# Hash attention and a squared-ReLU feed-forward: both feed-forward products by halves with seven products

## The chip, the cores and the metric

The kernel runs on one core of a Trainium2 chip. The metric is the device time of one execution in microseconds (us), and lower is better. A core has five engines that run side by side and wait for each other by semaphores: TensorE (PE in the profile, and PEld for its weight loads), VectorE (DVE), ScalarE (ACT), GpSimd (POOL) and SyncE (SP), whose queue issues nearly all transfers here. Products land in PSUM, which TensorE writes and VectorE and ScalarE read; all else lies in SBUF or in DRAM.

## The reference

```python
mask   = q_bucket[:, :, :, None] == k_bucket[:, :, None, :]   # 6 sign bits of q @ proj, k @ proj
scores = scale * q @ k.T;  scores = where(mask, scores, -1e9) - max
attn   = exp(scores) / (sum + 1e-9)
x      = (attn @ v).transpose(0, 2, 1, 3).reshape(3072, 512)   # 4 x 8 heads, 768 x 64
h      = x @ w_in          # 512 x 2048
g      = maximum(h, 0) ** 2
out    = g @ w_out         # 2048 x 512
```

Inputs and the result are float32, the two weights float64.

## The kernel before, in words

**First part, attention.** The 32 heads are worked on as 16 pairs, each pair on 128 partitions (64 a head), and each pair in six steps of 128 keys: 96 steps. A step has on TensorE the scores (`score`, L306: a bf16 product of sign bits that lifts the keys of the same bucket, then the float32 product of features, for queries 0 to 383 and then 384 to 767), one item that prepares the next pair (`features`, `hash_bits`), and the product with the values of the step before last (`attend`, L338). ScalarE takes the exponential (L313) into a ring of eight tiles. VectorE adds them up over the keys (`add_up`, L327, one step later). At the end of a pair `sum_up` (L355, tile `tot`) sums these totals over partitions on TensorE, VectorE makes reciprocals, `spread` (L378) hands them round, and `normalize` (L392) writes the pair's part of x into `x_t`, which holds all of x in SBUF (48 KB a partition), features on partitions.

Beside that the float64 weights come in 32 pieces of 128 x 512, one every three steps: SP loads a piece (`load_weight`), three steps later VectorE, GpSimd and ScalarE take it apart (`part_weight`), and a step after that it is rounded to float32 (`round_weight`; the last operation is a product on GpSimd, L159). `w_in` lies as four blocks of 128 rows, `w_out` as sixteen.

**Second part, feed-forward.** x is taken in six chunks of 512 tokens. The hidden stage of a chunk makes 16 tiles of 128 hidden units x 512 tokens, each from four products (L500), then ScalarE's ReLU out of PSUM (L506) and VectorE's square (L508). The output stage makes four tiles of 128 tokens x 512 features, each from 16 products (L517), copied out by ScalarE (L522) and written by SP. In chunks 1 and 2 VectorE also takes maxima of q and k (`peak`, L468), and in chunk 3 `guard` turns them into a flag (L483): were it set, a general path (`general`) would do all again. It isn't set here.

**What sets the order.** Each engine has a queue and works strictly in the order in which the program was written; the pools of tiles add the waits: a new tile waits until what lay in its memory before has been read.

Of the kernel before, what the change touches and what calls it, by code (L numbers as in the profile page):

```python
# [8 lines left out]
FP32 = mybir.dt.float32  # L9
# [5 lines left out]
ALU = mybir.AluOpType  # L15
# [18 lines left out]
def kernel(  # L34
# [24 lines left out]
    PIECE = 512  # L59
    assert (S, D, DM) == (768, 64, 512) and 3 * NBITS <= D  # L60
# [14 lines left out]
    fast = ExitStack()  # L75


    x_t = fast.enter_context(tc.tile_pool(name="x_all", bufs=1)).tile([P, NFT, B * S], FP32, name="x_t")

    first = ExitStack()  # L80
    p_qk = first.enter_context(tc.tile_pool(name="p_qk", bufs=2))
    p_f = first.enter_context(tc.tile_pool(name="p_f", bufs=2))
    p_w = first.enter_context(tc.tile_pool(name="p_w", bufs=2))
    p_v = first.enter_context(tc.tile_pool(name="p_v", bufs=3))
# [137 lines left out]
    def load_pair(pr, k_queue):  # L222
        b, j = divmod(pr, PB)
        tiles = []
        for src, pool, name in ((q, p_qk, "q_nat"), (k, p_qk, "k_nat"), (v, p_v, "v_nat")):
            pair = src[b, 2 * j:2 * j + 2]
            if src is v:
                t = pool.tile([P, 2, SB * D], FP32, name=name)
                nc.sync.dma_start(out=t, in_=pair.rearrange("h (p t) d -> p h (t d)", t=SB))
            else:  # L230
                t = pool.tile([P, SB, 2, D], FP32, name=name)
                for h in range(2):
                    (k_queue if src is k else nc.sync).dma_start(
                        out=t[:, :, h], in_=pair[h].rearrange("(p t) d -> p t d", t=SB)
                    )
            tiles.append(t)
        nat[pr] = tiles

    def features(pr, w, r):
# [4 lines left out]
        for i in range(SB // 2):  # L244
# [3 lines left out]
                in_=nat[pr][w][:, t].rearrange("p h d -> p (h d)"),  # L248
# [48 lines left out]
    def score(pr, kt):  # L297

        st = [ps_s.tile([P, 2, 512], FP32, name="st") for _ in range(2)]
        key = slice(kt * P, (kt + 1) * P)  # L300
        for c in range(2):
            cut = slice(c * HS, (c + 1) * HS)
            for src, first in ((bits, True), (feat, False)):
                for h in range(2):
                    rows = slice(h * D, (h + 1) * D)
                    nc.tensor.matmul(  # L306
                        out=st[h][:, c, 0:HS], lhsT=src[pr, 1][rows, key],
                        rhs=src[pr, 0][rows, cut], start=first, stop=not first,
                    )
        for h in range(2):  # L310
# [3 lines left out]
                out=e[:, 0:S].rearrange("p (c f) -> p c f", c=2), in_=st[h][:, :, 0:HS],  # L314
                func=ACTF.Exp, scale=scale,
# [15 lines left out]
    def attend(pr, kt):  # L331
        if kt == 0:
            outs[pr] = ps_o.tile([P, 2, 512], FP32, name="xo")
# [383 lines left out]
```

## Time and profile before

| | |
|---|---|
| median of three runs | 1065.76 us (1065.65 to 1066.94) |
| the profiled execution | 1067.2 us |
| its span, first to last instruction | 1065.4 us |
| mean granted clock of TensorE | 0.999 |
| busy: PE, DVE, ACT, POOL | 1046.3, 426.7, 285.0, 116.2 us |
| attention, weights beside it | 0 to 398.8 us |
| feed-forward, twelve stages | 398.9 to 1060.3 us |

A row of a group has the line, engine, operation, the tiles written and read, their shape and the count; behind the first bar the busy time in us and the mean of one in ns, behind the second the idle time of that engine just before and what ended it. A row of the timeline has start and length in us, engine, line, tiles, shape and count, and in brackets the wait. A float32 product is recorded as two passes, so counts of these are twice those in the code.

### The profile page before, as it was taken

Reading aid. Unit: us, or ns where it says so; the run is one execution under the profiler, and the core shown is the slowest. Engines: PE = TensorE matmul, PEld = TensorE weight load, DVE = VectorE, ACT = ScalarE, POOL = GpSimd, SP = SyncE. Lnnn points to the kernel's source line nnn. Section 1 sums busy time; section 2 is a strip of 40 time slices with the busy share of each in tenths; the row PEclk is TensorE's granted clock in tenths of the full one; section 3 lists DMA queues with packets and bytes.
Section 4 is the critical chain, followed back from the end, with each engine's and each line's share of the span. In section 5 each row is a group of like instructions: output and inputs, shape, how many; then the busy total and the mean of one; then the engine's idle time right before and its main releaser. Section 6 shows DMA issues by size and latency. Waiting matters only on the chain.

```text
span 1065.4 us, 10162 instructions
## 1 busy us (share of the span) xinstructions
PE 1046.3 (98%) x4066; PEld 456.0 (43%) x4066; DVE 426.7 (40%) x593; ACT 285.0 (27%) x457; POOL 116.2 (11%) x115
## 2 busy tenths in 40 slices
PE   6999999999999999999999999999999999999998
PEld 3444444444444434444444444444444444444443
DVE  2888888888888882200341034101210011001100
ACT  4555555555555541100110011001100111001100
POOL 1232322333232330000000000000000000000000
PEclk9999999999999999999999999999999999999999
DMA  8233333334421100000420033000000000000000
GB/s 198 81 93 85 85 86 84 85 114 119 104 85 55 61 20 0 1 10 20 157 89 10 20 128 119 10 20 10 1 0 20 20 1 0 20 20 1 0 20 22
DMA packets 65012, 55.24 MB, mean 52 GB/s; under 512 B 51648, under 2 KB 55744, under 8 KB 64960
## 3 DMA queue, kind: packets, MB, share of 16 engines
q1 hardware_dynamic: 63328, 54.14, 17.2%
q8 instruction: 34, 0.56, 0.2%
q10 hardware_dynamic: 1568, 0.39, 0.2%
q14 instruction: 18, 0.15, 0.0%
q0 software_dynamic: 64, 0.00, 0.0%
HBM read 48.24 MB, written 6.29 MB: 51 GB/s over the span
## 4 chain that ended last, share of the span: by engine, by line
PE 93%; DVE 3%; ACT 3%; issue 1%; DMA 1%; SPq 0%; ACTq 0%
PE hid L500 31%; PE y L517 31%; PE st L306 13%; PE xo L338 11%; ACT e L313 2%; PE tp L246 2%; PE near L263 2%; PE tot L355 1%; DVE flip L360 1%; DMA q_nat<-in_q_dram 1%; DVE one L131 0%; DVE power L127 0%; DVE once L366 0%; PE st L263 0%; DVE once L362 0%
## 5 line engine op out<-in xcount | busy, mean ns | idle before, releaser
L500 PE MATMUL hid<-x_t,w_in 128*128 128x512 f32 x768 | 330.8, 592 | 0.0
L517 PE MATMUL y<-w_out,gate 128*128 128x512 f32 x768 | 330.6, 592 | 0.0
L508 DVE TENSOR_TENSOR gate<-r 128x512 f32<-128x512 f32 x96 | 66.5, 692 | 508.9 <-ACT r L506 506.8
L517 PEld LDWEIGHTS y<-w_out,gate 128*128 128x128 f32 x768 | 145.9, 190 | 183.7 <-issue 183.4
L500 PEld LDWEIGHTS hid<-x_t,w_in 128*128 128x128 f32 x768 | 145.8, 190 | 183.3 <-issue 183.3
L313 ACT ACTIVATE e<-st 128x768 f32<-128x768 f32 x192 | 144.6, 805 | 89.3 <-PE st L306 89.3
L306 PE MATMUL st<-feat,feat 64*128 64x384 f32 x768 | 158.7, 485 | 0.0
L327 DVE TENSOR_TENSOR total<-total,e 128x768 f32<-128x768 f32 x128 | 145.6, 1186 | 1.5 <-ACT e L313 1.5
L338 PE MATMUL xo<-e,v_nat 128*64 128x384 f32 (+1 forms) x768 | 145.0, 499 | 0.0
L506 ACT ACTIVATE r<-hid 128x512 f32<-128x512 f32 x96 | 57.3, 597 | 275.4 <-PE hid L500 275.4
L522 ACT COPY o<-y 128x512 f32<-128x512 f32 x24 | 14.1, 586 | 315.7 <-PE y L517 315.7
L306 PEld LDWEIGHTS st<-feat,feat 64*128 64x128 f32 x768 | 69.4, 188 | 27.7 <-issue 27.2
L306 PE MATMUL st<-bits,bits 64*128 64x384 bf16 x384 | 71.7, 326 | 3.8 <-ACT e L313 1.9
L338 PEld LDWEIGHTS xo<-e,v_nat 128*64 128x64 f32 x768 | 46.6, 136 | 65.6 <-issue 65.5
L306 PEld LDWEIGHTS <-bits 64*128 64x128 bf16 x384 | 20.2, 93 | 69.3 <-issue 56.6
L327 DVE TENSOR_TENSOR total<-e,e 128x768 f32<-128x768 f32 x32 | 45.3, 1459 | 7.0 <-ACT e L313 7.0
L136 POOL TENSOR_SCALAR power<-power 128x512 uint32<-128x512 uint32 x32 | 22.9, 716 | 199.6 <-DVE power L127 199.6
L142 ACT ACTIVATE one<-one 128x512 f32<-128x512 uint32 x32 | 20.2, 630 | 84.9 <-DVE one L131 84.9
L159 POOL TENSOR_TENSOR w_in<-one,power 128x512 f32<-128x512 f32 x16 | 30.7, 1919 | 42.1 <-DVE one L156 42.1
L159 POOL TENSOR_TENSOR w_out<-one,power 128x512 f32<-128x512 f32 x16 | 30.0, 1878 | 41.2 <-DVE one L156 41.2
L251 ACT COPY feat<-tp 128x384 f32<-128x384 f32 x64 | 31.0, 484 | 5.4 <-PE tp L246 5.4
L139 POOL TENSOR_SCALAR power<-power 128x512 uint32<-128x512 uint32 x32 | 29.1, 910 | 2.6
(69 smaller groups left out, 373.0 us busy)
## 6 DMA issues: line engine op xcount, KB each, us to landing
raw<-in_moe_w_in_dram SPq DMA_DIRECT2D x16, 512.0 KB, 4.3
raw<-in_moe_w_out_dram SPq DMA_DIRECT2D x16, 512.0 KB, 3.8
q_nat<-in_q_dram SPq DMA_DIRECT2D x32, 192.0 KB, 5.1
v_nat<-in_v_dram SPq DMA_DIRECT2D x16, 384.0 KB, 3.2
out_dram<-o SPq DMA_DIRECT2D x24, 256.0 KB, 2.0
raw_qk<-in_q_dram SPq DMA_DIRECT2D x8, 768.0 KB, 4.2
raw_qk<-in_k_dram SPq DMA_DIRECT2D x8, 768.0 KB, 4.1
k_nat<-in_k_dram SPq DMA_DIRECT2D x30, 192.0 KB, 5.1
```

The costliest lines, as they stand in the source:

```text
L136: nc.gpsimd.tensor_scalar(out=power, in0=power, scalar1=1151.0, scalar2=896.0, op0=ALU.min, op1=ALU.max,)
L139: nc.gpsimd.tensor_scalar(out=power, in0=power, scalar1=-896.0, scalar2=2.0**23, op0=ALU.add, op1=ALU.mult,)
L159: nc.gpsimd.tensor_tensor(out=pieces[i][3], in0=one, in1=power.bitcast(FP32), op=ALU.mult)
L251: nc.scalar.copy(out=feat[pr, w][:, r * HS:(r + 1) * HS], in_=tp[:, 0:HS])
L306: nc.tensor.matmul(out=st[h][:, c, 0:HS], lhsT=src[pr, 1][rows, key], rhs=src[pr, 0][rows, cut], start=first, stop=not first,)
L313: nc.scalar.activation(out=e[:, 0:S].rearrange("p (c f) -> p c f", c=2), in_=st[h][:, :, 0:HS], func=ACTF.Exp, scale=scale,)
L327: nc.vector.tensor_tensor(out=totals[pr, h], in0=in0, in1=weights[pr, kt, h][:, 0:S], op=ALU.add)
L338: nc.tensor.matmul(out=xo[h * D:(h + 1) * D, c, 0:n], lhsT=nat[pr][2][:, h, kt * D:(kt + 1) * D], rhs=weights[pr, kt, h][:, c * HS:c * HS ...
L500: nc.tensor.matmul(out=hp, lhsT=w_in[:, ft, ff * P:(ff + 1) * P], rhs=x_t[:, ft, i * NCH:(i + 1) * NCH], start=(ft == 0), stop=(ft == NFT ...
L506: nc.scalar.activation(out=r, in_=hp, func=ACTF.Relu)
L508: nc.vector.tensor_tensor(out=g, in0=r, in1=r, op=ALU.mult)
L517: nc.tensor.matmul(out=y, lhsT=gates[ff][:, n * P:(n + 1) * P], rhs=w_out[:, ff], start=(ff == 0), stop=(ff == NFF - 1),)
```

## The change

**Second part.** Every operand is cut into halves both ways, and a product of two such operands is made from seven products of quarter blocks instead of eight, with sums of blocks ahead and sums of products behind. For the left operand these sums are S1 = A21 + A22, S2 = S1 − A11, S3 = A11 − A21, S4 = A12 − S2 (written over A21); for the right one T1 = B12 − B11, T2 = B22 − T1, T3 = B22 − B12, T4 = B21 − T2 (over B12). The seven products go into three accumulators of 256 columns, two of each kind: accumulator 0 takes A11·B11, S2·T2, S3·T3 and A22·T4 one after another, and ScalarE copies it out after each of the first three (`one`, `two`, `three`) before the next is added; accumulator 2 takes S1·T1, is copied (`five`), and then S4·B22; accumulator 1 holds A12·B21. VectorE adds the copies to make the four result blocks.

For x and w_in this gives four gate tiles of 128 x 256 per row of blocks (eight rows a chunk), and VectorE then makes the sums of the gates for the output product. GpSimd makes the sums of the weights: for `w_in` two rows of blocks near the end of attention (`sums_in`) and the other six in the first chunk, for `w_out` (`sums_out`) all eight in the first chunk. VectorE makes those of x (`load_x`). Since S4 and T4 are written over quarters of the weights, these quarters are first copied to DRAM (`kept_in`, `kept_out`) for the general path. The maxima of q and k come in sixteen pieces each of 768 columns over chunks 1 to 4, `guard` after the hidden stage of the last chunk.

**x through DRAM.** Each pair's x is normalized by one operation into a small tile and written to `x_all` in DRAM; a chunk of 512 tokens is read back by one transfer of 1 MB, the first while attention still runs, each other at the end of the hidden stage before.

**Attention.** Passes of 512 and 256 columns in place of two of 384 (scores) and 512 and 257 in place of 384 and 385 (output); the values are loaded one pair ahead into two buffers instead of three; weight pieces come every 2.7 steps instead of 3.

```diff
+    x_all = p_d.tile([P, NFT, B * S], FP32, name="x_all")
+    kept_in = p_d.tile([P, NFT // 2, DFF // 2], FP32, name="kept_in")
+    kept_out = p_d.tile([P, NFF // 2, DM // 2], FP32, name="kept_out")
...
-        for c in range(2):
-            cut = slice(c * HS, (c + 1) * HS)
+        for lo, hi in CUTS:
             for src, first in ((bits, True), (feat, False)):
...
-        for c in range(2):
-            cut = slice(c * HS, (c + 1) * HS)
-            nc.vector.scalar_tensor_tensor(
-                out=x_t[:, j, b * S + c * HS:b * S + (c + 1) * HS],
-                in0=xo[:, c, 0:HS], scalar=xo[:, 1, HS:HS + 1],
-                in1=recs[pr][:, cut], op0=ALU.add, op1=ALU.mult,
-            )
+        nc.vector.scalar_tensor_tensor(
+            out=x_t, in0=xo[:, 0:S], scalar=xo[:, S:S + 1],
+            in1=recs[pr], op0=ALU.add, op1=ALU.mult,
+        )
+        nc.sync.dma_start(out=x_all[:, j, b * S:(b + 1) * S], in_=x_t)
+
+    def sums_a(e, a11, a12, a21, a22, s1, s2, s3):
+        e.tensor_tensor(out=s1, in0=a21, in1=a22, op=ALU.add)
+        e.tensor_tensor(out=s3, in0=a11, in1=a21, op=ALU.subtract)
+        e.tensor_tensor(out=s2, in0=s1, in1=a11, op=ALU.subtract)
+        e.tensor_tensor(out=a21, in0=a12, in1=s2, op=ALU.subtract)
...
-    EVERY = 3
+    when = [27 * i // 10 for i in range(len(pieces))]
+    ROUNDED = when[-1] + 5
...
+            if u == ROUNDED:
+                early.close()
+                nc.sync.dma_start(out=kept_in, in_=w_in[:, 0:2, HF:DFF])
+                nc.sync.dma_start(out=kept_out, in_=w_out[:, 0:NR, HD:DM])
...
+                def load_x(i):
+                    x = p_c.tile([P, NFT, NCH], FP32, name="x")
+                    nc.sync.dma_start(out=x, in_=x_all[:, :, i * NCH:(i + 1) * NCH])
...
+                    sums_b(
+                        nc.vector, x[:, 0:2, lo], x[:, 0:2, hi], x[:, 2:4, lo], x[:, 2:4, hi], *t_x
+                    )
+                load_x(0)
+            if ROUNDED < u <= ROUNDED + 2:
+                sums_in(u - ROUNDED - 1)
...
+        def product(n, at, bt, c11, c12, c21, c22):
+            acc = [ps_m.tile([P, 512], FP32, name=f"acc{i}")[:, 0:HN] for i in range(3)]
...
+            add(0, at["11"], bt["11"], True, False)
+            one = keep(0, "one")
+            add(1, at["12"], bt["21"], True, True)
+            c11(acc[1], one)
+            add(0, at["s2"], bt["t2"], False, False)
+            two = keep(0, "two")
+            add(2, at["s1"], bt["t1"], True, False)
+            five = keep(2, "five")
+            add(0, at["s3"], bt["t3"], False, False)
+            three = keep(0, "three")
+            add(2, at["s4"], bt["22"], False, True)
+            c12(acc[2], two)
+            c22(three, five)
+            add(0, at["22"], bt["t4"], False, True)
+            c21(acc[0])
...
+            def gate(out):
+                def put(one, two=None):
+                    h = p_r.tile([P, HN], FP32, name="h", bufs=4)
+                    if two is None:
+                        nc.scalar.copy(out=h, in_=one)
+                    else:
+                        nc.vector.tensor_tensor(out=h, in0=one, in1=two, op=ALU.add)
+                    nc.vector.scalar_tensor_tensor(
+                        out=out, in0=h, scalar=0.0, in1=h, op0=ALU.max, op1=ALU.mult
+                    )
+                return put
+            product(2, at, bt, gate(g["11"]), gate(g["21"]), gate(g["12"]), gate(g["22"]))
+            sums_a(
+                nc.vector, g["11"], g["12"], g["21"], g["22"], g["s1"], g["s2"], g["s3"]
+            )
...
         for i in range(NCHUNK):
+            for r in range(NR):
+                if i == 0 and r + 2 < NR:
+                    sums_in(r + 2)
+                if i == 0:
+                    sums_out(r)
+                hidden(i, r)
+                if i > 0 and i < 5:
+                    peak(i % 2, (i - 1) // 2 * NR + r)
+            if i == NCHUNK - 1:
+                guard()
+            if i + 1 < NCHUNK:
+                load_x(i + 1)
+            for m in range(2):
+                project(i, m)
```

`keep` is a ScalarE copy out of an accumulator, `add` the products of one of the seven (two for a hidden block, eight for an output block), `project` the output product with `product(NR, ...)`.

Three places show how the instructions move. On TensorE, at the border of the two parts: before, the last `attend` of the last pair and then whole stages.

```order
L378 MATMUL tot<-both,picks 128x24
L338 MATMUL xo<-e_108,v_nat 64x384
L338 MATMUL xo<-e_109,v_nat 64x384
L338 MATMUL xo<-e_108,v_nat 64x385
L338 MATMUL xo<-e_109,v_nat 64x385
L500 MATMUL hid<-x_t,w_in 128x512 x64
L517 MATMUL y<-w_out,gate 128x512 x64
```

Now, at the same place, the first hidden row of blocks (`acc_3454`, `acc_3455` and `acc_3456` are its accumulators 0, 1 and 2; `t_x` and `s_in` are sums of x and of w_in):

```order
L344 MATMUL xo<-e_115,v_nat 64x257
L344 MATMUL xo<-e_116,v_nat 64x257
L534 MATMUL acc_3454<-x,w_in 128x256 x2
L534 MATMUL acc_3455<-x,w_in 128x256 x2
L534 MATMUL acc_3454<-t_x_3218,s_in_118 128x256 x2
L534 MATMUL acc_3456<-t_x_3217,s_in_117 128x256 x2
L534 MATMUL acc_3454<-t_x_3219,s_in_119 128x256 x2
L534 MATMUL acc_3456<-x,w_in 128x256 x2
L534 MATMUL acc_3454<-x,w_in 128x256 x2
L534 MATMUL acc_3510<-x,w_in 128x256 x2
```

Four products of 512 columns per hidden tile have become fourteen of 256 per row of blocks, which answers to two tiles; the first of them has a wait for the last normalization, since its accumulator lies where the attention output lay.

On VectorE, in pair 14 (steps 3 to 5): before, between the hash bits of pair 15 and the end of the pair.

```order
L270 TENSOR_SCALAR bits_2905<-far,bars,gains 64x384 x2
L127 TENSOR_SCALAR power<-raw 128x512
L131 TENSOR_SCALAR one<-raw 128x512
L327 TENSOR_TENSOR total_2835<-total_2835,e_104 128x768
L327 TENSOR_TENSOR total_2836<-total_2836,e_105 128x768
L152 SCALAR_TENSOR_TENSOR power<-raw,power 128x512
L156 SCALAR_TENSOR_TENSOR one<-raw,one 128x512
L327 TENSOR_TENSOR total_2835<-total_2835,e_106 128x768
```

Now:

```order
L279 TENSOR_SCALAR bits_3164<-far,bars,gains 64x384 x2
L160 SCALAR_TENSOR_TENSOR power<-raw,power 128x512
L164 SCALAR_TENSOR_TENSOR one<-raw,one 128x512
L334 TENSOR_TENSOR total_3084<-total_3084,e_115 128x768
L334 TENSOR_TENSOR total_3085<-total_3085,e_116 128x768
L417 TENSOR_TENSOR t_x_3217<-x 128x512
L418 TENSOR_TENSOR t_x_3219<-x 128x512
L419 TENSOR_TENSOR t_x_3218<-x,t_x_3217 128x512
L420 TENSOR_TENSOR x<-x,t_x_3218 128x2x256
L334 TENSOR_TENSOR total_3084<-total_3084,e_109 128x768
L334 TENSOR_TENSOR total_3085<-total_3085,e_110 128x768
```

The last rounding of a weight (L160, L164) has moved up to here, and the four sums of the first x chunk stand between the totals; the first of them waits for that chunk's transfer.

On GpSimd, at the end of the weights: before, the product of the last piece was the end of its work. Now that product is followed by the sums of `w_in`, then of `w_out` (`t_out`) and `w_in` in turn.

```order
L167 TENSOR_TENSOR w_out<-one,power 128x512
L411 TENSOR_TENSOR s_in_117<-w_in 128x2x128
L412 TENSOR_TENSOR s_in_119<-w_in 128x2x128
L413 TENSOR_TENSOR s_in_118<-s_in_117,w_in 128x2x128
L414 TENSOR_TENSOR w_in<-w_in,s_in_118 128x2x128
...
L417 TENSOR_TENSOR t_out_3417<-w_out 128x256
L418 TENSOR_TENSOR t_out_3419<-w_out 128x256
L419 TENSOR_TENSOR t_out_3418<-w_out,t_out_3417 128x256
L420 TENSOR_TENSOR w_out<-w_out,t_out_3418 128x256
L411 TENSOR_TENSOR s_in_117<-w_in 128x2x128
```

Twelve of these sums stand ahead of the first `t_out`, which waits for the last normalization and its transfer; 52 stand from there on.

212 lines of the change are left out of this document (134 added, 78 removed).

## The prediction

> **What bounds the kernel now.** I read the page first: busy shares, the chain that ended last, and the costliest groups.
>
> ```profile
> span 1065.4 us, 10162 instructions
> PE 1046.3 (98%) x4066; PEld 456.0 (43%) x4066; DVE 426.7 (40%) x593; ACT 285.0 (27%) x457; POOL 116.2 (11%) x115
> PE 93%; DVE 3%; ACT 3%; issue 1%; DMA 1%; SPq 0%; ACTq 0%
> L500 PE MATMUL hid<-x_t,w_in 128*128 128x512 f32 x768 | 330.8, 592 | 0.0
> L517 PE MATMUL y<-w_out,gate 128*128 128x512 f32 x768 | 330.6, 592 | 0.0
> ```
>
> TensorE is busy 98% and holds 93% of the chain; nothing is waited for before L500 and L517. Next the chain in order of time, for the second part:
>
> ```profile
> 398.90 55.13 PE hid L500 x128
> 454.03 54.93 PE y L517 x128
> ...
> 728.70 30.91 PE hid L500 x72
> 761.55 24.04 PE hid L500 x56
> ```
>
> Twelve stages of 54.93 us, 128 passes each (each fp32 product is recorded as two passes): 429.1 ns a pass. With the guard's hole (728.70 + 30.91 to 761.55, 1.94 us) the second part takes 398.9 to 1060.3, 661.4 us. Then the engines by stretch (PE, PEld, DVE, ACT, POOL busy, clock, DMA):
>
> ```profile
> 200.00:300.00 100.00, 99.77 (x663) 42.36 (x661) 87.45 (x117) 56.73 (x91) 30.29 (x25) 1.00 0.32 90
> 399.00:454.00 55.00, 55.00 (x129) 24.39 (x130) 12.68 (x19) 8.96 (x15) 1.27 (x1) 1.00 0.00 0
> ```
>
> Attention is TensorE-bound too, but with VectorE at 87%; the second part leaves every other engine idle. So a cut of TensorE work pays in full until a follower fills up.
>
> **The core: fewer, shorter passes.** Each block now needs 7 half-size products for 8. Hidden: 6 chunks × 8 rows × 7 products × 2 × 2 passes = 1344; output: 6 × 2 × 7 × 8 × 2 = 1344. All have 256 columns, which no full-array pass has now. Two things set a pass: its columns and the load of its weights.
>
> ```profile
> 500.22 0.19 PEld L517 LDWEIGHTS y<-w_out,gate 128*128 128x128 f32 x1 [0.24 <-issue]
> 500.65 0.19 PEld L517 LDWEIGHTS y<-w_out,gate 128*128 128x128 f32 x1 [0.24 <-issue]
> 166.62 0.33 PE L246 MATMUL tp<-ident,k_nat 128*128 128x128 f32 x1
> 166.78 0.38 PE L246 MATMUL tp<-ident,k_nat 128*128 128x128 f32 x2
> 166.89 0.27 PE L246 MATMUL tp<-ident,k_nat 128*128 128x128 f32 x1
> L246 PEld LDWEIGHTS tp<-ident,k_nat 128*128 128x128 f32 x96 | 11.5, 157 | 9.2 <-DVE power L152 7.6 <-DMA raw<-in_moe_w_in_dram 0.5 <-issue 0.5
> 7.23 1.51 PE L246 MATMUL tp<-ident,q_nat 128*128 128x128 f32 x6 [7.23 <-DMA q_nat<-in_q_dram]
> ```
>
> A load takes 0.19 us in a period of 0.43, beside the pass before it. The 128-column transposes, which have full loads of their own (x96 for 96), start at 166.62, 166.78 and 166.89: 0.11 to 0.16 us apart. Half of 429.1 is 214.6 ns and above both 0.16 and 0.19, so I take loads as hidden, and 215.8 ns a pass, an estimate that adds some 1.2 ns for a fixed part. 2688 × 0.2158 = 580.1 us (bounds: 576.8 with no fixed part; 645 at the 0.24 us that the first six transposes show, (1.51 − 0.30)/5).
>
> A rule of the Trainium skill speaks against this: "TensorE: Matmul & The Clock Gate", Part 3, What overlaps and what doesn't, has loads overlap only passes in other row groups. By it each full-array pass would carry its load in the open, and the second part would be about 2688 × (0.21 + 0.19) = 1075 us, where hidden loads give 580. The trace disagrees: a 512-column pass would then take 0.62 us, not the 0.43 between the two loads above, so I give that rule no chance of its own.
>
> **Does a product's inner chain fit?** One accumulator is copied out by ScalarE (L541 of the change) while TensorE does one other product of 4 passes (0.863 us) and then adds on to it.
>
> ```profile
> L251 ACT COPY feat<-tp 128x384 f32<-128x384 f32 x64 | 31.0, 484 | 5.4 <-PE tp L246 5.4
> 1057.51 2.74 PE L517 MATMUL y<-w_out,gate 128*128 128x512 f32 x6
> 1060.33 0.59 ACT L522 COPY o<-y 128x512 f32<-128x512 f32 x1 [13.15 <-PE y L517]
> 377.78 1.49 ACT L313 ACTIVATE e<-st 128x768 f32<-128x768 f32 x2
> 379.32 0.32 PE L306 MATMUL st<-bits,bits 64*128 64x384 bf16 x1 [0.38 <-ACT e L313]
> ```
>
> A copy takes 0.48 us at 384 columns and 0.59 at 512, so 0.38 at 256. A pass's end lies 0.16 us behind its columns (592 − 429), ScalarE starts 0.08 after that (1060.25 to 1060.33), TensorE 0.05 after ScalarE (379.27 to 379.32): 0.67 of 0.863 us. It fits with 0.19 to spare; each 0.1 us too little would cost 3 × 48 × 0.1 = 14 us.
>
> **VectorE in the hidden stage.** Per row of blocks, 11 operations of 256 columns (3 additions, 4 squarings, 4 sums), in four of six chunks a reduction of 768 too, against 28 × 0.2158 = 6.04 us of TensorE.
>
> ```profile
> L392 DVE SCALAR_TENSOR_TENSOR x_t<-xo,recs 128x384 f32<-128x384 f32 x32 | 18.4, 618 | 12.6 <-PE xo L338 12.6
> L152 DVE SCALAR_TENSOR_TENSOR power<-raw,power 128x512 uint32<-128x512 uint32 x32 | 21.9, 683 | 0.0
> L468 DVE TENSOR_REDUCE peaks<-raw_qk 128x1 f32<-128x1536 f32 x16 | 28.0, 1748 | 1.9 <-DMA raw_qk<-in_k_dram 1.0 <-DMA raw_qk<-in_q_dram 0.9
> ```
>
> At 1.04 ns a column (as from 512 to 1536) these give 0.485 us out of PSUM, 0.417 from SBUF, 0.95 for the reduction. 2 × 0.485 + 9 × 0.417 = 4.7, with the reduction 5.7: under 6.04. It is hidden, at 94%; with 0.6 us an operation it would not be.
>
> **First chunk: GpSimd and VectorE together.** GpSimd makes 64 sums of the weights, 256 columns each; 52 stand behind the last attention tile, since their tiles reuse its memory.
>
> ```profile
> L327 DVE TENSOR_TENSOR total<-total,e x128: 942/947/2037, 24.1 to 393.8; 128x768 f32<-128x768 f32 x128
> L159 POOL TENSOR_TENSOR w_out<-one,power x16: 1266/1918/1922, 226.0 to 401.4; 128x512 f32<-128x512 f32 x16
> 358.12 2.91 DVE L327 TENSOR_TENSOR total<-e,e 128x768 f32<-128x768 f32 x2
> 358.29 1.92 POOL L159 TENSOR_TENSOR w_out<-one,power 128x512 f32<-128x512 f32 x1 [3.16 <-DVE one L156]
> 360.95 1.81 DVE L327 TENSOR_TENSOR total<-total,e 128x768 f32<-128x768 f32 x2
> ```
>
> Two totals take 1.81 us alone and 2.91 beside one GpSimd product, which itself takes 1.92 for 1.27. So a GpSimd operation of 512 takes 1.1 us from VectorE, one of 256 half, 0.55; and lasts about 1 us. 52 × 0.55 = 28 us on top of 8 × 4.7: VectorE needs 64 to 66 us where TensorE needs 48.3. The output stage's first product wants its last gate 3.0 us after it starts (14 passes), and VectorE makes that gate some 3.7 us before its end: the stage starts at 66 − 3.7 − 3 = 59 for 48.3. I take 12 us, as VectorE also starts a product late; bounds 0 (the two engines miss each other) and 18 (no slack).
>
> The Trainium skill, "SBUF — State Buffer", Who interferes with whom, exempts VectorE operations with one SBUF input. No row here shows it; by it two of the eleven are free and the loss is some 2 us less.
>
> **The end of attention.** In the change VectorE's sums of the first x chunk stand between two totals of pair 14, and wait for a transfer of 1 MB that waits for GpSimd's last weight product.
>
> ```profile
> 363.39 1.37 DVE L270 TENSOR_SCALAR bits<-far,bars,gains 64x384 bf16<-64x384 f32 x2
> 365.47 2.65 DVE L327 TENSOR_TENSOR total<-total,e 128x768 f32<-128x768 f32 x2
> 374.29 0.85 PE L355 MATMUL tot<-total,ones 128*32 128x384 f32 x8
> v_nat<-in_v_dram SPq DMA_DIRECT2D x16, 384.0 KB, 3.2
> raw_qk<-in_q_dram SPq DMA_DIRECT2D x8, 768.0 KB, 4.2
> ```
>
> The bits end at 364.8, the last rounding (2 × 0.68) at 366.1, GpSimd's product at 368.0. 1 MB lands in some 5.2 us by 3.2 and 4.2, with its issue (some 0.3) at 373.5. Four sums of 512 (2.8 us) beside five of GpSimd's (2.7) end at 379; then four totals, 3.6 us: 382.6. TensorE wants them for L355 at 374.3 and waits, with the normalization and all scores behind it in its queue: 8 us; bounds 4 (no contention) and 12. The two 1 MB copies to DRAM ahead of it on SP wait for earlier weights only, so I charge nothing; if they queue before x, 12 is the price.
>
> Three smaller ones:
>
> ```profile
> DVE flip L360 <- PE tot L355: 31.1, 16, 2.3
> 398.83 0.70 PE L500 MATMUL hid<-x_t,w_in 128*128 128x512 f32 x1
> 398.95 1.15 DVE L392 SCALAR_TENSOR_TENSOR x_t<-xo,recs 128x384 f32<-128x384 f32 x2 [0.38 <-PE xo L338]
> 761.17 0.38 PE L483 MATMUL tp<-ident,top 128*1 128x128 f32 x2 [1.58 <-DVE top L477]
> ```
>
> Weight pieces come every 2.7 steps, not 3: some three pairs get a third piece (3.3 us of VectorE with its contention) where VectorE's slack before L355 is 1.1 us (1.94 of waiting, less 0.85 for the product itself); 4 us, bounds 0 and 7. L500 starts now before the last normalization; the change's first product waits for it: +1.2, less 0.8 that VectorE is quicker without roundings: +0.4. The guard's transposes stand behind the last sums, 3.3 us after TensorE: 4.0 us for 1.94.
>
> Edits at nothing: score and output passes of 512 + 256 columns hold the same columns as 384 + 384, and loads of 0.19 us for pairs of passes that share the array have the time of the two; if one showed at every 256, 96 steps × 0.05 = 5 us. One normalizing operation of 768 for two of 384 saves 0.2 us of a VectorE that is waited for little. The 16 writes of x tiles go on SP, each waiting for its normalization; behind them stand weight pieces that are wanted three steps (12 us) later, and DMA is at 0.32: no cost, else what a late piece adds to VectorE's queue. The next chunk of x is read and summed in some 9 us (0.3 + 5.2 + 2.8) of output stages that last 48; without that cover it would be 5 × 9.
>
> **Sum.** Second part 580.1 + 12 + 4.0 = 596.1 for 661.4: −65.3. Attention +8 + 4 + 0.4 = +12.4. Last copy −0.2. Together −53.1 on a span of 1065.4. That run took 1067.2 with its surroundings, the median of the runs is 1065.8; from the median, 1012.7: I say 1012 us.
>
> **Rivals.** *Costs hidden:* contention and stall mostly vanish: second part 576.8 + 4.0, so −80.6, attention +8: 993. For it: GpSimd's lone product is 1.27 us; against: 2.91 against 1.81. Chance 0.14. *VectorE binds:* at 0.55 us an operation 6.05 + 0.95 = 7.0 us a row against 6.04; 8 rows run up 7.7 us, 3 are borne by the two accumulators of each kind; about 5 × 4 chunks, and 10 more in the first: 1042. For it: 618 ns at 384 columns, dependent pairs; against: back-to-back totals at 905 ns a piece, below their 947. Chance 0.16. *Loads show at 256 columns, slower:* the load, not the columns, sets the pass. With the other terms above it decides from (661.4 − 28.2)/2688 = 0.236 us a pass; at 0.24 the second part takes 661, the whole 1078. For it: the six transposes at 7.23; against: those at 166.62. Chance 0.10. No change: 0.02. The forecast: 0.58.
>
> **Numbers.** Range 988 to 1038: below with the stall at 4, nothing in the first chunk and 576.8; above with 18, 12 and 7, and part of VectorE's rival. What a measurement here can tell from no change is about 0.2%. Faster 0.58 + 0.14 + 0.16 = 0.88, same 0.02, slower 0.10.
>
> **What would show it.** Right: 0.215 to 0.217 us between loads of a hidden stage; chunks two to six near 96.7 us each; a hole of about 8 us in TensorE before the tot product of pair 14; the first hidden stage at about 60 us with VectorE and GpSimd full. Wrong: hidden stages with TensorE waiting on VectorE or ScalarE in later chunks, passes above 0.23 us, or a first chunk like the others.

## The result, and the profile after

The changed kernel takes 1010.83 us (median of four runs, 1010.41 to 1011.51), the kernel before 1066.35 beside it (1065.65 to 1067.39). The ratio is 0.9479, 95% interval 0.9463 to 0.9496. The forecast was 1012.

The page of the changed kernel, span, busy shares and the groups that answer to those shown of before:

```profile
span 1009.3 us, 13406 instructions
PE 976.5 (97%) x5218; PEld 676.2 (67%) x5218; DVE 608.0 (60%) x1085; ACT 325.5 (32%) x637; POOL 182.4 (18%) x179
L534 PE MATMUL acc<-x,w_in 128*128 128x256 f32 x768 | 174.6, 379 | 1.2 <-issue 1.2
L534 PE MATMUL acc<-t_x,s_in 128*128 128x256 f32 x576 | 132.4, 379 | 3.9 <-ACT one L541 3.9
L541 ACT COPY one<-acc 128x256 f32<-128x256 f32 x60 | 22.3, 372 | 68.7 <-PE acc L534 68.7
```

TensorE is still the bound, with 70 us less busy time. A matmul row lasts 379 ns, but that includes the 0.16 us behind its columns; what a pass costs is read from a stage. Engines by stretch (length, then PE, PEld, DVE, ACT, POOL busy, granted clock, DMA share, GB/s): the stall, the stretch behind it, the first hidden stage, the first output stage, the second hidden stage.

```profile
380.40:388.20 7.80, 0.03 (x2) 0.00 (x0) 7.75 (x8) 0.03 (x1) 5.92 (x6) 0.72 0.00 1
388.20:394.30 6.10, 6.09 (x24) 2.18 (x24) 2.00 (x5) 0.37 (x1) 0.00 (x0) 0.52 0.00 0
415.40:468.40 53.00, 49.09 (x224) 42.16 (x225) 47.43 (x77) 14.18 (x39) 43.52 (x52) 1.00 0.02 8
468.40:516.70 48.30, 48.30 (x225) 42.53 (x224) 9.29 (x22) 3.72 (x10) 0.00 (x0) 1.00 0.11 39
516.70:565.10 48.40, 48.40 (x226) 42.59 (x225) 36.38 (x88) 14.89 (x40) 0.00 (x0) 1.00 0.24 71
```

An ordinary stage is 48.35 us for 224 passes, 0.2158 us a pass: the forecast's number. TensorE has no gap in it, and the loads stand beside the passes. The first hidden stage is 4.7 us longer, and attention has a stall with a slow clock (0.52) behind it. On TensorE's timeline three of the places where it waited (three waits inside the first hidden stage, 3.9 us together, are shown further down):

```profile
388.21 2.37 PE L361 MATMUL tot<-total,ones 128*32 128x384 f32 x8 [7.79 <-DVE total L334]
415.37 1.96 PE L534 MATMUL acc<-x,w_in 128*128 128x256 f32 x8 [1.17 <-issue]
954.89 0.38 PE L584 MATMUL tp<-ident,top 128*1 128x128 f32 x2 [2.86 <-DVE top L578]
```

The feed-forward part now begins at 415.37 (398.83 before) and TensorE ends at about 1003.5: attention +16.5 us, second part 588.1 for 661.4.

### The profile page after: what moved, and what is told of

It is laid out like the page before. It is cut to its first block, busy times and chain, and to the rows that moved or that the text cites. A ratio compares the mean times of both kernels' runs of the same rounds, so it can differ in the third digit from the quotient of the medians.

```text
span 1009.3 us, 13406 instructions
## 1 busy us (share of the span) xinstructions
PE 976.5 (97%) x5218; PEld 676.2 (67%) x5218; DVE 608.0 (60%) x1085; ACT 325.5 (32%) x637; POOL 182.4 (18%) x179
## 3 DMA queue, kind: packets, MB, share of 16 engines
q1 hardware_dynamic: 72416, 68.82, 23.9%
## 5 line engine op out<-in xcount | busy, mean ns | idle before, releaser
L534 PE MATMUL acc<-x,w_in 128*128 128x256 f32 x768 | 174.6, 379 | 1.2 <-issue 1.2
L534 PE MATMUL acc<-w_out,g 128*128 128x256 f32 x768 | 168.7, 379 | 0.0
L534 PEld LDWEIGHTS acc<-x,w_in 128*128 128x128 f32 x768 | 145.7, 190 | 21.5 <-issue 1.6
L534 PEld LDWEIGHTS acc<-w_out,g 128*128 128x128 f32 x768 | 145.8, 190 | 19.8
L314 PE MATMUL st<-feat,feat 64*128 64x512 f32 (+1 forms) x768 | 155.7, 489 | 0.0
L344 PE MATMUL xo<-e,v_nat 128*64 128x512 f32 (+1 forms) x768 | 145.0, 499 | 0.0
L534 PE MATMUL acc<-t_x,s_in 128*128 128x256 f32 x576 | 132.4, 379 | 3.9 <-ACT one L541 3.9
L534 PE MATMUL acc<-t_out,gs 128*128 128x256 f32 x576 | 126.3, 379 | 0.0
L534 PEld LDWEIGHTS acc<-t_x,s_in 128*128 128x128 f32 x576 | 109.1, 190 | 19.9 <-issue 3.1
L534 PEld LDWEIGHTS acc<-t_out,gs 128*128 128x128 f32 x576 | 109.4, 190 | 14.9
```

Of the source, the lines that this page charges most:

```text
L314: nc.tensor.matmul(out=st[h][:, lo:hi], lhsT=src[pr, 1][rows, key], rhs=src[pr, 0][rows, lo:hi], start=first, stop=not first,)
L344: nc.tensor.matmul(out=xo[h * D:(h + 1) * D, lo:hi], lhsT=nat[pr, "v_nat"][:, h, kt * D:(kt + 1) * D], rhs=weights[pr, kt, h][:, lo:hi], s ...
L534: nc.tensor.matmul(out=acc[to], lhsT=a(i), rhs=b(i), start=first and i == 0, stop=last and i == n - 1, skip_group_check=True,)
```

## The experiments

The kernel before was timed beside each of these, at 1066.0 to 1066.4 us (medians).

### The first x chunk summed four steps later

This run is called `x_sums_late`. The read of the first x chunk stays where it is; its four sums on VectorE move behind the last totals of pair 14.

```diff
...
                 load_x(0)
+            if u == ROUNDED + 4:
+                sum_x(0)
...
```

> The changed kernel, with the four VectorE sums of the first x chunk four steps later (behind the end of pair 14); the transfer itself stays where it is. Theory: TensorE's hole of 7.8 us before the tot product of pair 14 comes from these sums standing in VectorE's queue, and the half clock behind the hole costs another 3.2 us; both go, about 11 us, from 1010.8 to about 1000 us, and the tot product of pair 14 runs at full clock. Rival: VectorE is late there anyway (weight pieces every 2.7 steps), and the sums only move the hole to pair 15 or to the border of the two parts: 1006 to 1011 us.

Measured: 1001.96 us (1001.77 to 1002.43), ratio 0.9395 [0.938, 0.9411]: 8.9 us less than the change. TensorE's timeline at the end of pair 14:

```profile
378.46 1.51 PE L344 MATMUL xo<-e,v_nat 128*64 128x512 f32 x8
379.90 0.83 PE L361 MATMUL tot<-total,ones 128*32 128x384 f32 x2
380.92 0.85 PE L361 MATMUL tot<-total,ones 128*32 128x384 f32 x6 [0.18 <-DVE total L334]
```

The hole is gone, and so is the slow stretch behind it: the first hidden stage starts at 405.15, 10.2 us earlier. The end came only 8.6 us earlier, because the clock fell in another place (945.00:950.00 in this kernel, granted clock 0.66), right behind the guard's hole of 2.86 us. In the profile of the change the guard's hole, also 2.86 us long, had no such effect.

### GpSimd's weight sums left out of the first chunk

This run is called `no_weight_sums`. GpSimd leaves out 52 of the 64 sums of the weights and makes 39 fills with zeros in their place (39, not the 36 of the expectation), so TensorE still makes every product, but with wrong weight sums.

```diff
-                if i == 0 and r + 2 < NR:
+                if i == 0 and r == 0:
                     sums_in(r + 2)
+                if i == 0 and 0 < r < NR - 2:
+                    for t in s_in:
+                        nc.gpsimd.memset(t[:, :, (r + 2) * P:(r + 3) * P], 0.0)
                 if i == 0:
-                    sums_out(r)
+                    for t in t_out:
+                        nc.gpsimd.memset(t[:, r], 0.0)
```

> The changed kernel without GpSimd's 52 sums of weights in the first chunk (in their place 36 fills with zeros of the same size, which read nothing), so the feed-forward computes with wrong weight sums. Theory: the first hidden stage is longer than the others (53.0 against 48.35 us) only because these sums read SBUF beside VectorE; it becomes 48.35, the whole 1006 us, with VectorE at 0.42 us an operation there. Rival: VectorE starts late at the border, or the transfer of the second chunk disturbs it; the first stage stays near 53 us and the whole near 1011.

Measured: 1008.03 us (1005.16 to 1008.67). In the profiled execution (span 1003.4) the first hidden stage runs from 414.09 to 462.51, 48.42 us instead of 53.04. So 4.6 of the 4.7 us are the doing of GpSimd's sums, and no more than that: the term of 12 us was too large. The four runs differ by 3.5 us, and by and large the span grows as the mean granted clock falls: 1003.4 us at 0.996, 1006.8 at 0.993. The median shows only 2.8 of the 4.6 us. This kernel still has both holes on TensorE; that the clock behind them took the rest would fit the mean clocks, but only the fastest of the four runs has a trace, so it isn't shown.

### Weight pieces every 2.7 steps, alone

This run is called `before_pieces`: the kernel before with the change's schedule of weight pieces and nothing else.

```diff
-    EVERY = 3
+    when = [27 * i // 10 for i in range(len(pieces))]
...
```

> The kernel before with one part of the change: weight pieces every 2.7 steps instead of 3. In the changed kernel the tot product comes 5.3 us later by pair 13 than before. Theory: the denser weight pieces on VectorE do that; here too pairs 2, 3, 5, 7, 11 and 12 get 0.7 to 1.6 us longer and the whole is about 1071 us. Rival: the passes of 512 and 256 columns or the writes of x to DRAM do it; here then 1066 us as before.

Measured: 1072.86 us (1071.99 to 1073.25), ratio 1.0062 [1.0045, 1.0079]. The `tot` products of pairs 1, 2 and 3 in this kernel:

```profile
62.72 0.85 PE L355 MATMUL tot<-total,ones 128*32 128x384 f32 x8
87.45 0.85 PE L355 MATMUL tot<-total,ones 128*32 128x384 f32 x8
112.84 0.85 PE L355 MATMUL tot<-total,ones 128*32 128x384 f32 x8
```

Pairs of 24.7 and 25.4 us, against 24.6 and 25.3 in the change (starts at 63.33, 87.95 and 113.22) and 23.9 before: the schedule alone makes this loss, 4.8 us at the border of the two parts in the profile and 6.5 us between the medians. It is the term of 4 us (bounds 0 and 7).

### Passes of 512 and 256 columns and one normalization, alone

This run is called `before_cuts`: the kernel before with these two parts of the change. The cut below is that of the score passes; the output passes and the normalization are edited as in the change.

```diff
...
-        for c in range(2):
-            cut = slice(c * HS, (c + 1) * HS)
+        for lo, hi in CUTS:
...
```

> The kernel before with one part of the change: score and output passes of 512 and 256 columns and the normalization in one operation. Theory: the same columns, so the same time, 1066 us within 0.2% (perhaps 1 us less at the start, where the changed kernel was 0.7 to 0.9 us ahead in the first two pairs). Rival: a weight load shows at every pass of 256 columns of a pair of passes that share the array: 5 us more, 1071.

Measured: 1066.28 us (1065.62 to 1066.95, ten runs), ratio 0.9999 [0.9989, 1.0009]. The edit costs and gains nothing that these runs can tell, as the prediction had it.

### Hidden passes of 256, 128 and 64 columns, eight products

This run is called `narrow_passes`: the kernel before, and only its hidden stages are cut finer.

```diff
-                for ft in range(NFT):
-                    nc.tensor.matmul(
-                        out=hp, lhsT=w_in[:, ft, ff * P:(ff + 1) * P],
...
+                W = (256, 128, 64)[i // 2]
+                for c in range(0, NCH, W):
+                    for ft in range(NFT):
+                        nc.tensor.matmul(
+                            out=hp[:, c:c + W], lhsT=w_in[:, ft, ff * P:(ff + 1) * P],
...
```

> The kernel before, its hidden stages alone cut into passes of 256 columns (chunks one and two), 128 (three and four) and 64 (five and six); same columns, same results, 256, 512 and 1024 passes a stage. Theory (a load is hidden as long as the columns take longer than it): 256 columns give 0.2158 us a pass, 55.2 us a stage for 54.93 before; at 128 the columns alone would be 0.107, below the load's 0.15 to 0.19, so the load sets the pass: 0.11 at the least (56 us) and 0.16 at the most (82 us); at 64 the same load bounds it, so 0.11 to 0.16 us a pass, 112 to 160 us a stage. Rival (the load is added to each pass): 256 columns at 0.36 to 0.40 us, 92 to 102 us a stage.

Measured: 1190.85 us, one run. The chain that ended last, second part (start, length, engine, tile, line, passes): the hidden stages of chunks one, two, three and five, and one output stage.

```profile
398.62 55.45 PE hid L502 x256
454.07 54.93 PE y L519 x128
509.00 55.25 PE hid L502 x256
...
619.19 57.17 PE hid L502 x512
...
845.36 114.29 PE hid L502 x1024
```

At 256 columns a pass costs 55.25 / 256 = 0.2158 us, half of 512 columns and a little more: the load is hidden. At 128 it costs 57.17 / 512 = 0.1117, at 64 columns 114.29 / 1024 = 0.1116: half the columns save nothing, so here something other than the columns sets the pass, 0.112 us each. The load, of which each pass has one, is the likeliest, but nothing here separates it from other costs that come with every pass. The rows of the loads, 186 to 193 ns long, overlap one another, so their length isn't their period. The rival in which loads show at 256 columns had them at 0.24 us, twice what a pass takes here: there was room down to half the width that the change uses.

### Holes of four lengths

This run is called `clock_holes`: the kernel of `x_sums_late`, and behind four hidden stages one, two, four and seven dead additions on VectorE, whose result TensorE transposes before it goes on.

```diff
...
+            if 0 < i < NCHUNK - 1:
+                hole((1, 2, 4, 7)[i - 1])
...
```

> x_sums_late with a hole put on TensorE behind the hidden stage of chunks two, three, four and five: 1, 2, 4 and 7 dead VectorE additions of 768 columns (0.94 us each) stand behind the last sums, and TensorE transposes their result before it goes on. Holes of some 3.6, 4.6, 6.5 and 9.3 us are to come out. Theory (behind a long enough hole TensorE runs at half its clock for some 6 us, whatever the hole's length, and loses about 3 us): each of the longer ones costs its length and 3 us, about 1002 + 24 + 12 = 1038 us; if the shortest are below the length that matters, 1032. Rival 1 (the slow tot and spread products behind the hole of 7.8 us came of what VectorE and GpSimd did there, not of the clock): each hole costs its length alone, 1026 us, and the granted clock stays 1.00 behind it. Rival 2 (the loss grows with the hole): the hole of 9.3 us loses two to three times what that of 3.6 us does.

Measured: 1041.25 us, one run. TensorE's timeline at the five holes (the last is the guard's):

```profile
559.97 0.33 PE L608 MATMUL tp<-ident,idle 128*128 128x128 f32 x1 [4.51 <-DVE idle L606]
664.27 0.45 PE L608 MATMUL tp<-ident,idle 128*128 128x128 f32 x1 [5.59 <-DVE idle L606]
771.72 0.45 PE L608 MATMUL tp<-ident,idle 128*128 128x128 f32 x1 [7.58 <-DVE idle L606]
881.33 0.45 PE L608 MATMUL tp<-ident,idle 128*128 128x128 f32 x1 [10.55 <-DVE idle L606]
983.15 0.38 PE L589 MATMUL tp<-ident,top 128*1 128x128 f32 x2 [2.95 <-DVE top L583]
```

The output stages behind them are 50.0, 51.1, 50.3, 50.1 and 50.2 us long, where 48.4 is the length without a hole (48.5 for the last): 1.7, 2.7, 1.9, 1.7 and 1.7 us are lost behind holes of 4.5 to 10.6 and of 3 us. Stretches around the second hole:

```profile
660.70:663.30 2.60, 0.00 (x0) 0.00 (x0) 2.53 (x5) 0.00 (x0) 0.00 (x0) 1.00 0.96 362
663.30:670.10 6.80, 5.83 (x15) 4.69 (x16) 3.33 (x5) 0.00 (x0) 0.00 (x0) 0.50 0.01 4
670.10:675.00 4.90, 4.90 (x24) 4.33 (x23) 0.42 (x1) 0.37 (x1) 0.00 (x0) 1.00 0.00 0
```

Read in stretches of 0.1 us, the granted clock falls to one half 3.9 to 5.4 us after TensorE has stopped, and TensorE then works for 3.4 to 5.8 us at that clock. Behind the holes of 4.5 and 3 us the fall comes 0.8 and 1.0 us after TensorE is at work again. The loss is about half of the time at the low clock, and doesn't grow with the hole: the longest loses no more than the guard's. The four holes came to 28.2 us for 24 expected and the losses behind them to 8.0 for 12, so 1041 came near the 1038 of the expectation because two misses nearly cancelled. GpSimd is idle in these stretches, so it needs no GpSimd to make the slow stretch, and rivals 1 and 2 fall.

### The guard ahead of its stage's end

This run is called `early_guard`: `x_sums_late` with the guard's work moved.

```diff
...
+                if i == NCHUNK - 1 and r == 1:
+                    tops()
+                if i == NCHUNK - 1 and r == 4:
+                    guard()
                 hidden(i, r)
...
```

> x_sums_late with the guard's two reductions put ahead of the second row of the last hidden stage and its two transposes ahead of the fifth row. Theory (the hole is VectorE's last sums, which the transposes stand behind, and a short slow stretch of the clock follows it): the 2.9 us before the transposes go, and the 1.7 us that the last output stage took longer in that profile: 997 to 999 us. Rival (the output stage waits for the same sums by itself, the hole only moves): 1002 us.

Measured: 998.1 us (997.99 to 998.8), ratio 0.9358 [0.9342, 0.9374]. The guard's transposes and the start of the last output stage:

```profile
918.66 0.38 PE L591 MATMUL tp<-ident,top 128*1 128x128 f32 x2
...
943.05 1.24 PE L539 MATMUL acc<-w_out,g 128*128 128x256 f32 x5
```

No wait is left there, and the last hidden and output stages take 48.56 and 48.51 us instead of the 51.58 and 50.20 of `x_sums_late`. The output stage doesn't wait for the sums of the last row.

### Weight pieces back in their places, the last one at step 91

This run is called `early_rounding`: `early_guard` with another schedule of the weight pieces.

```diff
-    when = [27 * i // 10 for i in range(len(pieces))]
-    ROUNDED = when[-1] + 5
+    when = [2 * i if i < 5 else 3 * i - 5 for i in range(len(pieces))]
+    ROUNDED = when[-1] + 4
...
```

> early_guard with weight pieces in the places they have before (two a pair, at the same two steps), but for the first five, which come every two steps; the last one is rounded at step 91 of 96 instead of 87, and the first x chunk is summed at step 95. Theory (a piece off its place adds VectorE work to a pair that has 1.1 us of slack; 13 pairs lost 5.3 us so): some 5 us of it come back, less 1 for the third piece of the second pair: 993 to 994 us. Rival 1 (the pairs are longer for another reason): 998 us. Rival 2 (the x chunk, now two steps before the end of attention, is summed too late and the first hidden product waits): 1000 us or more.

Measured: 1003.19 us (1001.04 to 1004.29), ratio 0.94 [0.9384, 0.9416]: 5 us more than `early_guard`, not 4 to 5 less. VectorE and TensorE at the end of the last pair:

```profile
383.76 2.91 DVE L334 TENSOR_TENSOR total<-e,e 128x768 f32<-128x768 f32 x2
386.59 8.49 DVE L334 TENSOR_TENSOR total<-total,e 128x768 f32<-128x768 f32 x6
395.01 1.21 DVE L417 TENSOR_TENSOR t_x<-x 128x512 f32<-128x512 f32 x1
...
399.54 2.87 DVE L334 TENSOR_TENSOR total<-total,e 128x768 f32<-128x768 f32 x2
```
```profile
401.06 1.34 PE L361 MATMUL tot<-total,ones 128*32 128x384 f32 x2 [4.37 <-DVE total L334]
```

The stretch at the low clock (columns as in the stretches above):

```profile
401.20:414.90 13.70, 11.09 (x30) 5.51 (x30) 5.46 (x9) 0.37 (x1) 2.70 (x5) 0.50 0.07 29
```

Rival 2's time came about, and its cause, sums of x too late, but not its wait: TensorE waited ahead of the last pair's `tot` product, and not ahead of the first hidden one. The pairs themselves did go back to 23.9 us, but for the first two after the start (26.8 and 24.7). Then GpSimd's sums of w_in, which follow the last rounding, ran beside the totals of the last pair (1.4 us a total for 0.9), the sums of x stood ahead of the last two, and TensorE stopped for 4.37 us. The clock behind it stayed at one half for 13.7 us, 11.1 of them with TensorE at work, so some 5.5 us were lost, the largest such loss here; two more waits of 1.38 and 1.17 us lie in that stretch. It reached into the first hidden stage (54.66 us long for 53.04). The order of pieces was right and the place of the sums wrong.

### The extra pieces in the first pair, the last one at step 88

This run is called `pieces_at_start`: `early_guard` with a third schedule of the weight pieces.

```diff
-    when = [2 * i if i < 5 else 3 * i - 5 for i in range(len(pieces))]
-    ROUNDED = when[-1] + 4
+    parted = [(0, 1, 3, 4)[i] if i < 4 else 3 * i - 6 for i in range(len(pieces))]
+    ROUNDED = parted[-1] + 2
...
```

> early_guard with weight pieces in the two steps a pair that they have before, but for four in the first pair (the first two loaded ahead of the steps); the last one is rounded at step 88, and the first x chunk is summed at step 93, one step later than in early_guard and two earlier than in early_rounding. Theory (a third piece in a later pair is what costs, 0.7 to 1.6 us each, and sums two steps earlier than in early_rounding keep the last totals in time): pairs of 23.9 us, the first hidden stage starts some 4 us earlier than in early_guard, less 1 for the first pair, no hole ahead of the last tot product: 994 to 996 us. Rival 1 (four pieces in the first pair delay it by 3 us, as the third piece of the second pair did in early_rounding): 997 to 998 us. Rival 2 (the last totals are late again, with a hole of 4 us and a slow clock behind it): 1000 us or more.

Measured: 994.34 us (993.2 to 994.58), ratio 0.9327 [0.9314, 0.9339]. `tot` products of pairs 1 to 3, and of the last pair:

```profile
65.72 0.85 PE L361 MATMUL tot<-total,ones 128*32 128x384 f32 x8
89.61 0.85 PE L361 MATMUL tot<-total,ones 128*32 128x384 f32 x8
113.50 0.85 PE L361 MATMUL tot<-total,ones 128*32 128x384 f32 x8
...
395.23 0.90 PE L361 MATMUL tot<-total,ones 128*32 128x384 f32 x8
```

Pairs of 23.9 us and no hole; the first hidden stage starts at 400.53, within 1.7 us of where it starts before the change.

### One squaring of a row on ScalarE in the first chunk

This run is called `squares_on_scalar`: `pieces_at_start` with one operation of each row moved.

```diff
...
+                    if i == 0 and two is None:
+                        h = p_r.tile([P, HN], FP32, name="h", bufs=4)
+                        nc.scalar.activation(out=h, in_=one, func=ACTF.Relu)
+                        nc.scalar.activation(out=out, in_=h, func=ACTF.Square)
+                        return
...
```

> pieces_at_start with one of the four squarings of a row moved from VectorE to ScalarE in the first chunk alone: the accumulator that has no second term is read by a Relu and squared by a second activation instead of a copy and a VectorE operation. Theory (the first hidden stage is 4.7 us longer than the others because VectorE, slowed by GpSimd's sums, is late; one of eleven operations a row less gives it 8 x 0.4 to 0.9 us): 3 to 4.7 us less than pieces_at_start. Rival (the extra activation stands in ScalarE's queue ahead of the next product's first copy, which TensorE's third block waits for): no gain, or up to 3 us more.

Measured: 989.84 us (989.33 to 990.87), ratio 0.9286 [0.9274, 0.9299], 4.5 us less than `pieces_at_start`. The first hidden stage of `pieces_at_start` and of `squares_on_scalar`:

```profile
400.50:453.50 53.00, 49.07 (x224) 42.19 (x225) 47.38 (x76) 14.19 (x39) 43.51 (x52) 1.00 0.02 8
```
```profile
401.00:449.80 48.80, 48.60 (x224) 42.31 (x225) 42.60 (x66) 17.39 (x46) 43.57 (x52) 1.00 0.02 9
```

VectorE works 4.8 us less, ScalarE 3.2 more, GpSimd the same, and the stage is 48.86 us long instead of 53.03. A row still takes VectorE 6.94 us beside GpSimd (426.70 to 433.64 in this kernel), more than TensorE's 6.04, so VectorE still falls behind; what went is TensorE's waiting for it, 3.9 us before and 0.2 now. The edit does two things at once: it takes work from VectorE, and it lets ScalarE itself free the `h` tile that it wants next. Which of them counts more wasn't separated. This is the shortest of all kernels here: 21 us below the change, 7.1% below the kernel before.

## Why the prediction came out

**The core was right to a tenth of a per cent.** 0.2158 us a pass was forecast and measured, and twelve stages of 48.35 us make 580.2 for the 580.1 of the forecast; the finer cut of the kernel before shows the same pass with eight products. So the fall of time is the product count, 7 for 8, and nothing else in the second part helped. The rival in which loads show fell with it: its price of 0.24 us a pass came from the first six transposes of the program, and the 0.112 us measured for a pass of 128 or 64 columns is the low end of the later ones (0.11 to 0.16). Why the first six were slower stays open. The rival in which VectorE binds fell too: a row takes it 4.2 us alone and a reduction 0.95 (945 ns in the page's group), together 5.1 of TensorE's 6.04, and no later hidden stage is longer than 48.35.

**The inner chain fits.** The copies took 372 ns (forecast 380), and TensorE waited for one three times in 48 rows, all in the first chunk, where the copy itself was late.

**The first chunk was mis-sized and put in the wrong place.** The step was: VectorE needs 64 to 66 us, and the output stage then waits for its last gate, 12 us. In the trace the output stage waits for nothing. TensorE waits inside the hidden stage, three times for 3.9 us in all, and the chain is longer than I had it: VectorE is late with a square, so one of four `h` tiles isn't free, so ScalarE's copy into it stands in its queue ahead of the next row's `one`, which TensorE wants. ScalarE, TensorE and then VectorE in the change:

```profile
448.15 0.37 ACT L622 COPY h<-acc 128x256 f32<-128x256 f32 x1 [3.64 <-DVE g L625]
448.42 0.38 ACT L541 COPY one<-acc 128x256 f32<-128x256 f32 x1
```
```profile
448.94 2.83 PE L534 MATMUL acc<-t_x,s_in 128*128 128x256 f32 x12 [1.39 <-ACT one L541]
456.74 2.83 PE L534 MATMUL acc<-t_x,s_in 128*128 128x256 f32 x12 [1.52 <-ACT one L541]
464.02 2.83 PE L534 MATMUL acc<-t_x,s_in 128*128 128x256 f32 x12 [0.99 <-ACT one L541]
```
```profile
440.18 0.94 DVE L411 TENSOR_TENSOR gs<-g,g 128x256 f32<-128x256 f32 x1
443.65 0.41 DVE L624 TENSOR_TENSOR h<-acc,one 128x256 f32<-128x256 f32 x1
447.98 0.94 DVE L411 TENSOR_TENSOR gs<-g,g 128x256 f32<-128x256 f32 x1
...
463.06 0.41 DVE L411 TENSOR_TENSOR gs<-g,g 128x256 f32<-128x256 f32 x1
...
467.23 0.42 DVE L411 TENSOR_TENSOR gs<-g,g 128x256 f32<-128x256 f32 x1
```

A row of VectorE takes 447.98 − 440.18 = 7.8 us beside GpSimd and 467.23 − 463.06 = 4.2 alone (4.7 forecast). 43.5 us of GpSimd are 5.6 such rows, so contention costs 5.6 × 3.6 = 20 us where I had 28, and the eight rows need 8 × 4.2 + 20 = 54, where I had 65. That is an estimate from these rows. Put into the forecast's own sum, 54 − 3.7 − 3 = 47 us, it would have cost the output stage nothing; the 4.7 us that were lost come from the chain through ScalarE, which the forecast didn't have. The sum that reads PSUM and SBUF (443.65) keeps its 0.41 us beside GpSimd while those with two SBUF inputs take 0.94. This is the exemption in the Trainium skill, "SBUF — State Buffer", Who interferes with whom: the trace agrees. I had given it 2 us; how much of the 8 us it accounts for, no run separates. The run with one squaring fewer on VectorE shows the chain by its cure: ScalarE's wait for VectorE falls from 12.5 to 3.5 us, and TensorE's for ScalarE from 3.9 to 0.2.

**The stall was right, what followed it was missed.** 8 us were forecast for the hole, 7.79 measured, and by its steps: x landed 5.4 us after its issue (5.2 forecast, where a straight line through the two rows it came from gives 4.9), its sums and the totals ran beside GpSimd. The two copies to DRAM ahead of it had landed by 371.8 us and x was issued at 374.9, so they cost nothing, as forecast. VectorE in the change:

```profile
380.42 0.69 DVE L417 TENSOR_TENSOR t_x<-x 128x512 f32<-128x512 f32 x1 [4.72 <-DMA x<-x_all]
381.03 1.21 DVE L418 TENSOR_TENSOR t_x<-x 128x512 f32<-128x512 f32 x1
...
384.42 4.60 DVE L334 TENSOR_TENSOR total<-total,e 128x768 f32<-128x768 f32 x4
```

But the prediction had no term for the clock. Behind the hole TensorE ran 6.1 us at a clock of 0.52 (the second stretch above), which loses 0.48 × 6.1 = 2.9 us; from `tot` to the end of `spread` it took 6.05 us (388.21 to 394.26) and before the change 2.83 (374.29 to 377.12). The run with holes shows that this is the clock and not the stall's contention: GpSimd is idle there.

**The small terms.** Weight pieces 4 forecast, 4.8 to 6.5 measured (`before_pieces`: at the border, and between the medians). Border 0.4 forecast, the first product's wait 1.17. Guard 4.0 forecast, 3.2 measured, with 1.7 of slow clock behind it in `x_sums_late` and `clock_holes`. Cuts of 512 and 256 columns: nothing, as forecast.

**The sum.** Second part 588.1 us for 596.1 forecast, attention +16.5 for +12.4: the first chunk was 7 us too dear and attention 4 us too cheap, and these partly cancelled. In the span, where all terms were read, the forecast was 1065.4 − 53.1 = 1012.3 us and 1009.3 was measured. That the medians differ by 1 us only is luck in part: the sum was taken from a median that lay 1.4 us below the profiled run of the kernel before, while the change's median lies 0.2 below its own. The lower end of the range, 988, doesn't follow from the terms named for it, which give 1012.7 − 3.3 − 12 − 4 = 993. The mechanisms were right but for the missing clock and the wrong place of the first chunk's wait; of the single costs the first chunk's, 12 us for 4.7, was the farthest off.

## What to carry to other kernels

Fewer products pay in full where TensorE is the bound and each pass stays longer than the shortest spacing of passes with loads of their own, which is here 0.112 us; find that spacing by halving the columns until the time stops falling, not from the length of a load's row. What could be won beyond it, 21 us, lay in its seams: sums standing in VectorE's queue ahead of something that TensorE waited for, weight work out of step with the pairs, and two engines reading SBUF at once. Each of these was mended by moving instructions and not by removing any, and each move had to be tried, since one of them (the last rounding four steps later, in `early_rounding`) opened a hole in a new place.

## What the runs showed of the hardware

**A hole costs more than its length.** Behind the start of the program, a wait of TensorE of 4.4 us or more was each time followed by half the clock. It cost 1.7 to 2.9 us beyond itself in `clock_holes` and in the change, independent of its length, and some 5.5 us in `early_rounding`, where two short waits followed. A wait of 2.9 us was followed by half the clock in two profiled executions (`x_sums_late`, `clock_holes`) and not in two others (the change, `no_weight_sums`). The Trainium skill, "TensorE: Matmul & The Clock Gate", Part 1: The HAM clock gate, has a free-running window of 3.4 us and half rate after an idle one. The trace agrees for the longer holes, where the fall comes 3.4 (the change) to 5.4 us after the stop. By that rule alone a hole of 2.9 us would be too short, and two runs show it isn't always.

**Loads come closer together than they are long.** In `narrow_passes` they are 0.112 us apart with rows of 0.19, and passes of 64 columns are no cheaper than those of 128. A reading of 0.19 as the load's cost would have put the narrowest pass that costs only its columns at some 225 columns (0.19 us by 0.843 ns a column, the 215.8 ns of 256); by 0.112 us it is some 130. Both are estimates.

**Still open.** The wait of 1.17 us ahead of the first hidden product, in all kernels with seven products, was not tried. By the code it is there because the accumulator takes the place of the attention output, and in the change the last normalization ends at 415.26 us, 0.1 us before that product; the trace itself names no releaser. How much of the spread between runs of one kernel (3.5 us in `no_weight_sums`) comes from where the clock's fall lies was read from the mean clock alone.
